# Sliding-window attention and highway layer on one core: a list-scheduled order of the pieces, one ring of two-bank PSUM buffers, x transposed by DMA, masks and normalising by head pairs

## The chip, the core and the metric

One core of one Trainium2 chip runs the whole program. The metric is device time in microseconds (us). Engines are named as in the profile: PE (matmul) with PEld (its weight loads), DVE, ACT, POOL, and SP, which here only issues DMAs. Each engine works through its own instructions in the order in which they were written, and waits at an instruction until what it needs is done.

## What is computed

Eight batches, eight heads, 576 positions, head size 64; the attention output, with the heads side by side, is the input x of a highway layer over 4608 rows of 512.

```python
scores = scale * np.matmul(q, k.transpose(0, 1, 3, 2))
bias = slopes[:, None, None] * (-np.abs(rel).astype(np.float32))[None, :, :]
mask = (rel >= 0) & (rel < window)          # rel = query - key, window = 128
scores = np.where(mask, scores + bias[None], -1000000000.0)
attn = softmax(scores)
x = (attn @ v), heads side by side: [B * S, H * D]
H = np.maximum(x @ w_h, 0.0)
T = 1.0 / (1.0 + np.exp(-(x @ w_t + b_t)))
out = T * H + (1.0 - T) * x
```

## The kernel before

**Tiling.** Two batches form a *pair* m (0 to 3). A pair has two *stages*: s = 0 covers its first 256 queries, s = 1 the other 320 (with a tail of 64). A *unit* u is one head of one stage, for both batches: 4 x 2 x 8 = 64 units. The eight stages are also numbered st = 0 to 7. A *block* b is 128 rows of x; an even stage has four, an odd one five (the fifth holds both tails), 36 in all.

**A unit's chain.** `transposes` (L188) brings q and k of two heads (a group hp, 16 transposes on PE into one `pt` tile) into QT and KT, copied by DVE (q, L204) and ACT (k, L209); a fifth group does the tails (L218). `scores` (L236, matmuls L254) fills a two-bank PSUM tile `sc` (two of them), `soft` (L264) takes the exponential on ACT, `mask` (L273) multiplies by a 0/1 mask with the distance factor on DVE. `pv` (L290) multiplies with v, which has a column of ones behind it, into `av`, and `norm` (L315, L316) divides by that column's sum into x, on DVE. `av` has one buffer.

**A block's chain.** `f_xt`: four PE transposes of x (L326) into a `pt` tile, of which there is one for all transposes in the kernel, copied to `xt` by ACT (L332). `f_h`: four matmuls with w_h (L340) and, on DVE, `uu = max(h, 0) - x` (L344). `f_z`: four matmuls with w_t (L353) and one that adds the bias from a single row (L355), tanh on ACT (L358), and `tt = 0.5 tt + 0.5` on POOL (L359). `f_g`: `uu = uu * tt` on DVE (L364), called the gate product below. `f_out`: `ot = uu + x` on POOL (L368), then four (or two) stores issued by SP (L380, L374).

**Order.** A loop written out by hand (L415 to L459) sets one order for all engines. Slot u writes the exponential of unit u, the scores of u + 1, the mask of u - 1, a share of the previous stage's block steps, product and norm of u - 2, more block steps, and from the sixth slot of a pair on one transpose group of the next pair. The gate product and the sum of a block are written one step after its z. POOL also issues all loads (they convert float32 to bfloat16): those of pair 0 and the weights first, then those of pair m + 1 in the first nine slots of pair m. At most eight of POOL's loads are in flight: the next issue waits for the eighth before it.

Of the kernel before, what the change touches and what calls it, by code (L numbers as in the profile page):

```python
# [10 lines left out]
P = 128  # L11
# [3 lines left out]
def kernel(  # L15
# [10 lines left out]
    nc = tc.nc  # L26
    B, H, S, D = q.shape
# [13 lines left out]
    NU = ND * 2 * H  # L41
# [4 lines left out]
    p0p = ctx.enter_context(tc.tile_pool(name="p0", bufs=11))  # L46
    p1p = ctx.enter_context(tc.tile_pool(name="p1", bufs=4))
    smp = ctx.enter_context(tc.tile_pool(name="small", bufs=4))
    xp = ctx.enter_context(tc.tile_pool(name="x", bufs=2))
    fx = ctx.enter_context(tc.tile_pool(name="fx", bufs=3))  # L50
# [47 lines left out]
    def load_v(m, cs):  # L98
# [11 lines left out]
    load_qk(0, slice(0, 2))  # L110

    ident = cp.tile([P, P], BF16, name="ident")
    nc.vector.memset(ident[:], 1.0)
    nc.gpsimd.affine_select(
        out=ident[:], in_=ident[:], compare_op=ALU.is_equal, fill=0.0,
        base=0, pattern=[[1, P]], channel_multiplier=-1,
    )
    kk_i = cp.tile([P, 1], I32, name="kk_i")
    nc.gpsimd.iota(kk_i[:], pattern=[[0, 1]], base=0, channel_multiplier=1)

    load_v(0, (0, 1))
    load_qk(0, slice(2, 4))
    load_qk(0, slice(4, 8))


    M0 = cp.tile([P, H, 512], BF16, name="m0")
    M1 = cp.tile([P, H, 512], BF16, name="m1")
    tri = cp.tile([P, 3, P], BF16, name="tri")
    nc.vector.memset(tri[:], 1.0)
    nc.gpsimd.affine_select(  # L130
        out=tri[:, 0, :], in_=tri[:, 0, :], compare_op=ALU.is_ge, fill=0.0,
        base=0, pattern=[[1, 4], [4, 32]], channel_multiplier=-1,
    )
    nc.gpsimd.affine_select(
        out=tri[:, 1, :], in_=tri[:, 1, :], compare_op=ALU.is_ge, fill=0.0,
        base=-1, pattern=[[-1, 4], [-4, 32]], channel_multiplier=1,
    )
    nc.gpsimd.affine_select(
        out=tri[:, 2, 0:D], in_=tri[:, 2, 0:D], compare_op=ALU.is_ge, fill=0.0,
        base=-1, pattern=[[-1, D]], channel_multiplier=1,  # L140
    )
    nc.gpsimd.affine_select(
        out=tri[:, 2, D:P], in_=tri[:, 2, D:P], compare_op=ALU.is_ge, fill=0.0,
        base=0, pattern=[[1, D]], channel_multiplier=-1,
    )
    kk_f = cp.tile([P, 1], F32, name="kk_f")
    nc.vector.tensor_copy(out=kk_f[:], in_=kk_i[:])
    BIAS = cp.tile([P, H], F32, name="bias")
    for h in range(H):
        nc.vector.tensor_scalar(  # L150
            out=BIAS[:, h : h + 1], in0=kk_f[:, 0:1],
            scalar1=slopes[h], scalar2=None, op0=ALU.mult,
        )
    hb = lambda n: [P, H, n]

    def bc(ap, n):
        return ap.rearrange("p (o n) -> p o n", o=1).to_broadcast(hb(n))

    for off in (0, 256):
        nc.vector.tensor_copy(out=M0[:, :, off : off + P], in_=bc(tri[:, 0, :], P))  # L160
    for off in (0, 256):
        nc.vector.tensor_copy(out=M1[:, :, off : off + P], in_=bc(tri[:, 0, :], P))
    nc.vector.tensor_copy(out=M1[:, :, 448:512], in_=bc(tri[:, 2, D:P], D))
    for h in range(H):
        c_h = float(np.exp(-float(P) * slopes[h]))
        for M, off, n, s in ((M0, 128, P, 1), (M0, 384, P, 1), (M1, 128, P, 1), (M1, 384, D, 2)):
            nc.vector.tensor_scalar(  # L167
                out=M[:, h, off : off + n], in0=tri[:, s, 0:n],
                scalar1=c_h, scalar2=None, op0=ALU.mult,
            )  # L170
    for i in range(2):
        nc.vector.memset(VA[i][:, :, :, :, D : D + 1], 1.0)
        nc.vector.memset(VA[i][D:P, 4, :, :, :], 0.0)
        nc.vector.memset(KT[i][:, :, S : 5 * P], 0.0)
    ones1 = cp.tile([1, P], BF16, name="ones1")
    nc.vector.memset(ones1[:], 1.0)

    load_tails(0)
    wH = cp.tile([P, NCK, DM], BF16, name="wH")
    wT = cp.tile([P, NCK, DM], BF16, name="wT")  # L180
    bT = cp.tile([1, DM], BF16, name="bT")
    nc.gpsimd.dma_start(out=wH[:], in_=moe_w_h.rearrange("(c p) n -> p c n", p=P))
    nc.gpsimd.dma_start(out=wT[:], in_=moe_w_t.rearrange("(c p) n -> p c n", p=P))
    nc.gpsimd.dma_start(out=bT[:], in_=moe_b_t.rearrange("(o n) -> o n", o=1))
    load_v(0, (2, 3, 4))
# [303 lines left out]
```

## Time and profile before

| | us |
|---|---|
| median of three runs | 243.84 |
| lowest, highest | 243.78, 250.88 |
| the profiled execution | 247.06 |
| its span, first to last instruction | 245.3 |

The span is what the views of the profile divide up; the small rest of an execution lies around it. In rows that group instructions, the fields are: line, engine, operation, tiles written and read, count, then busy us and mean ns of one, then the idle time of the engine ahead of them and what ended it. Rows of the waits: the waiting engine and line, what it waited for, us in total, times, longest. Rows in order of time: start, duration, engine, line and operation, with idle time and its cause in brackets. Matmuls overlap in the pipeline, so what one costs is read from start to start.

### The profile page before, as it was taken

The page shows a single profiled execution, that of the slowest core. Times are in us where ns is not written, and L with a number is a line of the kernel's source. Part 1 is how long each engine was busy: PE and PEld are TensorE (multiplying, and loading weights), DVE is VectorE, ACT ScalarE, POOL GpSimd, SP SyncE. Part 2 cuts the span into 40 slices and gives each one's busy share as a digit, 9 for nine tenths or more (in the row PEclk, how much of TensorE's full clock was granted, in tenths as well). Part 3 has the DMA queues.
Part 4 walks back from the last instruction along what each step waited for, and adds up shares of the span by engine and source line. Part 5 has one row for each costly group of instructions (what it writes and reads, how often), then busy time and mean ns, then how long its engine had stood idle before and what let it go on. Part 6 is the DMA issues. An engine that isn't in the chain of part 4 may idle for free.

```text
span 245.3 us, 5032 instructions
## 1 busy us (share of the span) xinstructions
PE 177.5 (72%) x2004; PEld 96.5 (39%) x2004; DVE 142.1 (58%) x339; ACT 126.3 (51%) x157; POOL 119.1 (49%) x139
## 2 busy tenths in 40 slices
PE   1355702498898777868887986888887997887980
PEld 1133402376553334445533343455443344533430
DVE  4169501364677656565786575365786586785340
ACT  2324610185665756447675645646656766562440
POOL 8987733300245876531257784412233356223572
PEclk9999965556999999799999798879999999999996
DMA  5999999995019999930159999530113223122243
GB/s 61 135 191 190 167 129 198 143 108 12 6 41 157 217 199 163 104 73 17 45 81 217 208 155 127 67 74 0 45 43 77 54 56 78 43 63 69 52 112 92
DMA packets 70199, 24.97 MB, mean 102 GB/s; under 512 B 48160, under 2 KB 65568, under 8 KB 70176
## 3 DMA queue, kind: packets, MB, share of 16 engines
q0 software_dynamic: 63392, 15.21, 80.5%
q1 hardware_dynamic: 6784, 9.45, 15.3%
q8 instruction: 15, 0.25, 0.4%
q14 instruction: 8, 0.07, 0.1%
HBM read 30.41 MB, written 9.44 MB: 162 GB/s over the span
## 4 chain that ended last, share of the span: by engine, by line
POOL 34%; issue 25%; DMA 16%; DVE 9%; PE 8%; ACT 3%; SPq 2%; POOLq 1%; ACTq 0%
POOL ot L368 16%; DMA kl<-in_k_dram 8%; POOL tt L359 8%; DMA out_dram<-ot 5%; DVE uu L364 5%; POOL va L102 4%; DMA ql<-in_q_dram 3%; PE pt L197 3%; SPq L380 2%; PE av L290 2%; DVE m L167 1%; POOL ktl L93 1%; PE sc L254 1%; ACT xt L332 1%; POOL kl L73 1%
## 5 line engine op out<-in xcount | busy, mean ns | idle before, releaser
L264 ACT ACTIVATE pt<-sc,bias 128x1024 bf16<-128x1024 f32 x64 | 71.0, 1118 | 0.7 <-PE sc L254 0.7
L359 POOL TENSOR_SCALAR tt<-tt 128x512 f16<-128x512 f16 x36 | 22.2, 618 | 85.8 <-ACT tt L358 77.7
L368 POOL TENSOR_TENSOR ot<-uu,x 128x512 f32<-128x512 bf16 x36 | 44.5, 1235 | 19.6 <-DVE uu L364 16.3
L273 DVE TENSOR_TENSOR pt<-pt,m 128x1024 bf16<-128x1024 bf16 x64 | 52.2, 816 | 0.0
L364 DVE TENSOR_TENSOR uu<-uu,tt 128x512 bf16<-128x512 bf16 x36 | 15.3, 426 | 52.4 <-POOL tt L359 52.4
L290 PE MATMUL av<-va,pt 128*128 128x65 bf16 (+1 forms) x576 | 32.7, 205 | 13.8 <-DVE x L316 12.1
L358 ACT ACTIVATE tt<-pz 128x512 f16<-128x512 f32 x36 | 21.5, 597 | 39.3 <-PE pz L355 38.1
L340 PE MATMUL pa<-wH,xt 128*128 128x512 bf16 x144 | 39.8, 401 | 1.3 <-ACT xt L332 0.8
L353 PE MATMUL pz<-wT,xt 128*128 128x512 bf16 x144 | 38.9, 394 | 0.0
L290 PEld LDWEIGHTS <-pt 128*128 128x128 bf16 (+1 forms) x576 | 24.7, 105 | 33.7 <-DVE x L316 22.2
L332 ACT COPY xt<-pt 128x512 bf16<-128x512 bf16 x36 | 21.1, 586 | 31.2 <-PE pt L326 31.0
L209 ACT COPY kt<-pt 128x1024 bf16<-128x1024 bf16 x16 | 16.2, 1012 | 39.4 <-PE pt L197 39.4
L254 PE MATMUL sc<-qt,kt 64*128 64x256 bf16 (+2 forms) x384 | 29.6, 260 | 7.2 <-ACT kt L209 4.4
L316 DVE TENSOR_TENSOR x<-av,rd 128x256 bf16<-128x256 f32 (+1 forms) x64 | 29.3, 458 | 6.0 <-POOL ot L368 3.8
L197 PE MATMUL pt<-ident,ql 128*64 128x128 bf16 x256 | 13.3, 255 | 22.5 <-DMA ql<-in_q_dram 13.4
L102 POOL DMA_DIRECT2D va<-in_v_dram x20 | 22.2, 1113 | 12.6 <-DMA kl<-in_k_dram 4.5
L344 DVE SCALAR_TENSOR_TENSOR uu<-pa,x 128x512 bf16<-128x512 f32 x36 | 24.6, 682 | 5.3 <-PE pa L340 5.3
L326 PE MATMUL pt<-ident,x 128*128 128x128 bf16 x144 | 15.2, 228 | 8.4 <-DVE qt L204 4.2
L254 PEld LDWEIGHTS <-kt 64*128 64x128 bf16 x384 | 14.8, 100 | 15.9 <-issue 6.4
L197 PEld LDWEIGHTS <-ql 128*64 128x64 bf16 x256 | 10.6, 131 | 25.4 <-DMA ql<-in_q_dram 19.2
L204 DVE COPY qt<-pt 128x1024 bf16<-128x1024 bf16 x16 | 11.0, 689 | 15.2 <-PE pt L197 15.2
L340 PEld LDWEIGHTS <-xt 128*128 128x128 bf16 x144 | 11.7, 100 | 15.4 <-issue 4.5
(45 smaller groups left out, 129.1 us busy)
## 6 DMA issues: line engine op xcount, KB each, us to landing
out_dram<-ot SPq DMA_DIRECT2D x128, 64.0 KB, 1.7
va<-in_v_dram POOLq DMA_DIRECT2D x16, 256.0 KB, 8.7
ql<-in_q_dram POOLq DMA_DIRECT2D x3, 1024.0 KB, 11.1
kl<-in_k_dram POOLq DMA_DIRECT2D x3, 1024.0 KB, 12.3
out_dram<-ot SPq DMA_DIRECT2D x8, 128.0 KB, 2.4
ql<-in_q_dram POOLq DMA_DIRECT2D x4, 128.0 KB, 4.8
kl<-in_k_dram POOLq DMA_DIRECT2D x4, 128.0 KB, 5.3
ql<-in_q_dram POOLq DMA_DIRECT2D x2, 256.0 KB, 7.2
```

What stands on the lines that cost most here:

```text
L102: nc.gpsimd.dma_start(out=VA[i][0:n, c, :, :, 0:D].rearrange("s r h d -> s (r h) d"), in_=v[2 * m : 2 * m + 2, :, c * P : c * P + n, :].re ...
L197: nc.tensor.transpose(out=pt[r * D : (r + 1) * D, hl * 512 + t * P : hl * 512 + (t + 1) * P], in_=L[:, r, 2 * hp + hl, t * D : (t + 1) * D ...
L254: nc.tensor.matmul(out=sc[:, r, off : off + w], lhsT=KT[i][rows, h, j * P : (j + 1) * P], rhs=rhs, start=True, stop=True,)
L264: nc.scalar.activation(out=pt[:], in_=SC.pop(u)[:], func=ACTF.Exp, bias=BIAS[:, h : h + 1], scale=scale,)
L273: nc.vector.tensor_tensor(out=pt[:], in0=pt[:], in1=mk.to_broadcast([P, 2, 512]), op=ALU.mult,)
L290: nc.tensor.matmul(out=av[rows, g, :], lhsT=pt[:, r, off : off + w], rhs=va[:, j, r, h, :], start=n == 0, stop=n == len(terms) - 1,)
L316: nc.vector.tensor_tensor(out=x[:, 0:nb, h * D : (h + 1) * D], in0=av[:, 0:nb, 0:D], in1=rd[:, 0:nb].to_broadcast([P, nb, D]), op=ALU.mult,)
L340: nc.tensor.matmul(out=pa[:], lhsT=xt[:, c, :], rhs=wH[:, c, :], start=c == 0, stop=c == NCK - 1)
L353: nc.tensor.matmul(out=pz[:], lhsT=xt[:, c, :], rhs=wT[:, c, :], start=c == 0, stop=False)
L359: nc.gpsimd.tensor_scalar(out=tt[:], in0=tt[:], scalar1=0.5, scalar2=0.5, op0=ALU.mult, op1=ALU.add)
L364: nc.vector.tensor_tensor(out=uu[:], in0=uu[:], in1=TT.pop((st, b))[:], op=ALU.mult)
L368: nc.gpsimd.tensor_tensor(out=ot[:], in0=UU.pop((st, b))[:], in1=X[st][:, b, :], op=ALU.add)
```

## The change

**Order.** The hand-written loop goes. Every piece of work (a transpose group, its copy, the scores, the exponential, a mask, a product, a norm, each step of a block, each load, each constant) becomes a node with an engine, a cost in ns, a due time (units are due 2300 ns apart) and the nodes that it needs. A list scheduler in the kernel's Python keeps a clock for each engine and takes, again and again, the piece that can start first; among those that can start within 100 ns of the first on an engine it takes the one due first. It models loads (bytes per ns, eight in flight) and the PSUM ring. The resulting order is written out. A load is issued when its buffer is free in that model and POOL comes to it.

**PSUM.** One ring of four two-bank buffers `ps` serves scores, products, transposes (q in one bank, k in the other, so one buffer for both) and blocks (h in one bank, z in the other), taken strictly in order.

**x by DMA.** `f_x` issues one DMA transpose of a block, 128x512 bf16, from x to `xt`, on SP; the PE transposes L326 and the copies L332 are gone. `xt` has five buffers, x three, `ot` four of its own.

**Pairs.** Mask, product and norm work on two heads (w = u // 2): 32 masks of 128x2048 in place of 64 of 128x1024, 32 norms in place of 64, 32 reciprocals. One mask table `mk` serves both stages. The bias matmul uses 128 rows, of which all but the first are zero. Setup moves: ident and tri to POOL alone, the distance bias to ACT, and four of pair 0's five k copies from ACT to DVE.

Three places in the order. DVE, in the first stage of pair 1: before, masks (L273) of one head, norms (L315, L316) and the gate products (L364) alternate.

```order
L364 TENSOR_TENSOR uu<-uu,tt 128x512
L273 TENSOR_TENSOR pt_1006<-pt_1006,m_124 128x1024
L315 RECIPROCAL rd<-av 128x4
L316 TENSOR_TENSOR x<-av,rd 128x4x64
L273 TENSOR_TENSOR pt_1054<-pt_1054,m_124 128x1024
L344 SCALAR_TENSOR_TENSOR uu<-pa,x 128x512
```

And now (L298 is the mask, L342 and L343 the norm, L368 the `uu` of h, L393 the gate product):

```order
L368 SCALAR_TENSOR_TENSOR uu<-ps,x 128x512
L342 RECIPROCAL rd<-ps 128x2x4
L343 TENSOR_TENSOR x<-ps,rd 128x2x4x64
L298 TENSOR_TENSOR pt_907<-pt_907,mk 128x2048
L393 TENSOR_TENSOR uu<-uu,tt 128x512
L298 TENSOR_TENSOR pt_965<-pt_965,mk 128x2048
L368 SCALAR_TENSOR_TENSOR uu<-ps,x 128x512
```

The pieces are twice as long, and where the gate product stands between them follows from the scheduler's clocks instead of a fixed lag of one step.

POOL, from the first tt on, before (L359 and L368 are tt and ot, the rest are loads of pair 2):

```order
L359 TENSOR_SCALAR tt<-tt 128x512
L368 TENSOR_TENSOR ot<-uu,x 128x512
L73 DMA ql_91<-in_q_dram 128x16x256
L359 TENSOR_SCALAR tt<-tt 128x512
L368 TENSOR_TENSOR ot<-uu,x 128x512
L73 DMA kl_93<-in_k_dram 128x16x256
```

And now (L388 and L397 are tt and ot; ql_82 to ktl_88 and va_90 belong to pair 2, ql_83 and kl_85 to pair 3):

```order
L388 TENSOR_SCALAR tt<-tt 128x512
L397 TENSOR_TENSOR ot<-uu,x 128x512
L75 DMA ql_82<-in_q_dram 128x16x256
L75 DMA kl_84<-in_k_dram 128x16x256
L95 DMA qtl_86<-in_q_dram 64x8x64 x2
L95 DMA ktl_88<-in_k_dram 64x8x64 x2
L388 TENSOR_SCALAR tt<-tt 128x512
L75 DMA ql_83<-in_q_dram 128x16x256
L397 TENSOR_TENSOR ot<-uu,x 128x512
L75 DMA kl_85<-in_k_dram 128x16x256
L388 TENSOR_SCALAR tt<-tt 128x512
L104 DMA va_90<-in_v_dram 128x16x64 x2
```

Pair 2's and pair 3's loads of q and k now stand among the first three blocks.

SP, from its start, now:

```order
L353 DMA_TRANSPOSE xt<-x 128x4x128 x4
L413 DMA out_dram<-ot 32x512 x8
L353 DMA_TRANSPOSE xt<-x 128x4x128 x3
L413 DMA out_dram<-ot 32x512 x4
L353 DMA_TRANSPOSE xt<-x 128x4x128 x2
```

Where SP held stores alone, each block's transpose now stands among the stores of earlier blocks.

The core of the diff:

```diff
-    ps_sc = ctx.enter_context(tc.tile_pool(name="ps_sc", bufs=2, space=PSUM))
-    ps_tr = ctx.enter_context(tc.tile_pool(name="ps_tr", bufs=1, space=PSUM))
-    ps_av = ctx.enter_context(tc.tile_pool(name="ps_av", bufs=1, space=PSUM))
-    ps_a = ctx.enter_context(tc.tile_pool(name="ps_a", bufs=1, space=PSUM))
-    ps_z = ctx.enter_context(tc.tile_pool(name="ps_z", bufs=1, space=PSUM))
+    NPS = 4
+    psp = ctx.enter_context(tc.tile_pool(name="ps", bufs=NPS, space=PSUM))
+    def ps_tile(dt=F32):
+        return psp.tile([P, 2, 512 if dt == F32 else 1024], dt, name="ps")
...
+    EV = {
+        (m, w, hp): "ACT" if w and (m or hp == 0) else "DVE"
+        for m in range(ND) for w in (0, 1) for hp in range(5)
+    }
...
-        pt = ps_tr.tile([P, 1024], BF16, name="pt")
+        if w == 0:
+            TR[m, hp] = ps_tile(BF16)
+        pt = TR[m, hp][:, w, :]
...
+    def mask(w):
+        m, s, h = unit(2 * w)
+        n = 2 - s
+        o = PT[w][:].rearrange("p h r (j w) -> p h (r j) w", j=n)
+        mk = MK[:, h : h + 2, 0 : 512 // n].rearrange("p h (o w) -> p h o w", o=1)
+        nc.vector.tensor_tensor(
+            out=o, in0=o, in1=mk.to_broadcast([P, 2, 2 * n, 512 // n]), op=ALU.mult,
+        )
...
+        av = AV.pop(w)[:, :, 0 : nb * (D + 1)].rearrange("p h (b d) -> p h b d", b=nb)
+        rd = smp.tile([P, 2, 5, 1], F32, name="rd")
+        nc.vector.reciprocal(out=rd[:, :, 0:nb], in_=av[:, :, :, D : D + 1])
+        nc.vector.tensor_tensor(
+            out=x.rearrange("p b (h d) -> p h b d", h=2), in0=av[:, :, :, 0:D],
+            in1=rd[:, :, 0:nb].to_broadcast([P, 2, nb, D]), op=ALU.mult,
         )
...
-    def f_xt(st, b):
-        pt = ps_tr.tile([P, 1024], BF16, name="pt")
-        for c in range(NCK):
-            nc.tensor.transpose(
...
+    def f_x(st, b):
         xt = fx.tile([P, NCK, P], BF16, name="xt")
         XT[st, b] = xt
+        nc.sync.dma_start_transpose(out=xt[:], in_=X[st][:, b, :])
     def f_h(st, b):
         xt = XT[st, b]
-        pa = ps_a.tile([P, DM], F32, name="pa")
+        az = ps_tile()
+        pa, PZ[st, b] = az[:, 0, :], az[:, 1, :]
...
+    def node(key, eng, cost, prio, emit, deps=(), take=False, free=None, land=0):
...
+            for b in range(nb):
+                t = base + b * dt
+                kb = (st, b)
+                node(("x", kb), "SP", 700, t - 1.3 * dt, lambda kb=kb: f_x(*kb), alln, land=0.01)
+                node(("h", kb), "PE", 870, t, lambda kb=kb: f_h(*kb), [("x", kb), ("w", 0)], take=True)
+                node(("u", kb), "DVE", 690, t + 0.2 * dt, lambda kb=kb: f_u(*kb), [("h", kb)], free=("h", kb))
+                node(("z", kb), "PE", 1100, t + 0.5 * dt, lambda kb=kb: f_z(*kb), [("h", kb), ("w", 1), ("w", 2)])
+                node(("th", kb), "ACT", 600, t + 0.6 * dt, lambda kb=kb: f_th(*kb), [("z", kb)], free=("h", kb))
+                node(("t", kb), "POOL", 630, t + 0.6 * dt, lambda kb=kb: f_t(*kb), [("th", kb)])
+                node(("g", kb), "DVE", 430, t + 0.9 * dt, lambda kb=kb: f_g(*kb), [("u", kb), ("t", kb)])
+                node(("o", kb), "POOL", 1200, t + 1.0 * dt, lambda kb=kb: f_out(*kb), [("g", kb)])
...
+        if land and e == "POOL":
+            t = max(t, lanes[0] + SYNC)
+        if take and len(slots) >= NPS:
+            left, at = allocs[slots[-NPS]]
+            if left:
+                return None
+            t = max(t, at + SYNC)
...
+            t0 = min(c[0] for c in cands)
+            soon = [c for c in cands if c[0] <= t0 + LOOK]
+            c = min(soon, key=lambda c: c[1])
...
+    order.sort(key=lambda o: o[0])
     with tc.manual_schedule():
...
+        for t, key in order:
+            nodes[key][3]()
```

More of the change, by code (lines that the diff above doesn't have):

```diff
@@ L138 @@
[L138 to L170, printed above, removed]
@@ L309, in norm @@
+        if s == 1:
+            for hl in range(2):
+                for r in range(2):
+                    group(hl, 4, r, ((me, 384, 3), (me, 448, 4)), slice(r * D, (r + 1) * D))
+    def norm(w):
+        m, s, h = unit(2 * w)
         nb = NBLK[s]
@@ new lines, with start_of @@
+    ready = {e: [] for e in clock}
+    for key, nd in nodes.items():
+        if not waiting[key]:
+            ready[nd[0]].append(key)
+    def start_of(key):
+        e, cost, prio, emit, deps, take, free, land = nodes[key]
+        t = clock[e]
+        for d in deps:
+            t = max(t, when[d] + (0 if nodes[d][0] == e and not nodes[d][7] else SYNC))
+        if land and e == "POOL":
[5 more added lines that the diff above has]
+            t = max(t, at + SYNC)
+        return t
```

436 lines of the change are left out of this document (264 added, 172 removed).

## Prediction

> **What bounds the kernel now.** I read the page's engine line first, then busy time by stage, then who waits for whom on the busiest engines, then the start and end of the program in order of time.
>
> ```profile
> span 245.3 us, 5032 instructions
> PE 177.5 (72%) x2004; PEld 96.5 (39%) x2004; DVE 142.1 (58%) x339; ACT 126.3 (51%) x157; POOL 119.1 (49%) x139
> ```
>
> No engine is full over the span, so the average names no bound. Cut into start, middle and end (busy time by stage: PE, weight loads, DVE, ACT, POOL, then granted clock, DMA share, GB/s):
>
> ```profile
> 0.00:62.00 62.00, 30.70 (x405) 21.53 (x405) 27.54 (x96) 22.89 (x24) 31.42 (x45) 0.78 1.93 132
> 62.00:230.00 168.00, 138.47 (x1567) 71.61 (x1562) 110.03 (x235) 99.22 (x127) 79.21 (x85) 0.96 0.66 91
> 230.00:245.30 15.30, 8.32 (x43) 3.33 (x40) 4.53 (x9) 4.15 (x7) 8.48 (x10) 0.84 0.39 94
> ```
>
> Start and end leave PE more than half or almost half idle. In the middle 168 us PE is busy 138.5 and idle 29.5. The waits of that stretch, DVE's first, then PE's:
>
> ```profile
> DVE uu L364 <- POOL tt L359: 44.9, 31, 2.9
> DVE x L316 <- POOL ot L368: 3.8, 4, 1.0
> DVE uu L344 <- PE pa L340: 3.2, 4, 1.7
> DVE qt L204 <- PE pt L197: 2.8, 3, 1.2
> ...
> PE av L290 <- DVE x L316: 12.1, 22, 1.1
> PE pt L197 <- ACT xt L332: 5.6, 9, 0.7
> PE pt L326 <- DVE qt L204: 3.9, 4, 1.6
> PE pt L326 <- DVE qt L225: 3.9, 2, 1.9
> ```
>
> DVE's busy 110.0 plus these waits of 54.7 make 164.7 of 168: DVE, in its written order, sets the pace there, and 45 us of its time is standing at the gate product (L364) until POOL has made tt, with masks and norms behind it that are ready. PE's idle time is the echo: 12.1 us for the norm that frees the only `av` buffer, 13.4 us for the only `pt` buffer of all transposes.
>
> The start is a second bound:
>
> ```profile
> 30.19 0.36 PE L290 MATMUL av<-va,pt 128*128 128x65 bf16 x6
> 40.52 1.06 PE L197 MATMUL pt<-ident,ql 128*64 128x128 bf16 x16 [9.97 <-DMA ql<-in_q_dram]
> 46.21 1.06 PE L197 MATMUL pt<-ident,kl 128*64 128x128 bf16 x16 [2.38 <-DMA kl<-in_k_dram]
> ...
> 50.00:54.00 4.00, 4.00 (x66) 3.39 (x63) 3.26 (x9) 3.31 (x5) 0.00 (x0) 0.50 4.57 126
> 54.00:58.00 4.00, 3.75 (x53) 2.93 (x50) 2.58 (x5) 2.22 (x3) 0.00 (x0) 0.50 1.86 25
> 58.00:62.00 4.00, 3.33 (x45) 2.06 (x43) 1.51 (x4) 2.84 (x4) 0.00 (x0) 0.80 0.01 0
> ```
>
> PE stops for pair 1's q at 30.5 and really starts with its k at 46.2 (each after its load). It then runs at a granted clock of 0.50 although busy 7.75 of the 8 us from 50 to 58; the next 4 us have 0.80, so half speed lasts until about 59.
>
> **The change part by part.** The start: the loads ahead of pair 1's k are the same bytes, in nearly the same order (six q/k pieces for pair 0 become four, q and k each). POOL now makes ident and tri ahead of the second pieces; these are some 2 us of POOL, and the loads queue eight deep behind it. I keep 46.2, with 44 to 49 as ends. The new order has scores of fifteen of pair 0's units, six of its eight head-pair products with v and the first gate block on PE ahead of pair 1's transposes, where before seven units and no block stood; that work fills the 10 us hole, and leaves less for afterwards. Cover gone (pair 1 arriving earlier), it would cost its own time and the sum would not change.
>
> PE's work after 46.2, by its pace in a stretch where it hardly waits. Each row's start to the next row's start is the cost:
>
> ```profile
> 67.45 0.64 PE L197 MATMUL pt<-ident,ql 128*64 128x128 bf16 x16 [0.67 <-ACT xt L332]
> 68.02 0.40 PE L254 MATMUL sc<-qt,kt 64*128 64x256 bf16 x8
> 68.35 1.04 PE L353 MATMUL pz<-wT,xt 128*128 128x512 bf16 x4
> 69.32 0.39 PE L355 MATMUL pz<-bT,ones 1*128 1x512 bf16 x1
> 69.64 0.60 PE L290 MATMUL av<-va,pt 128*128 128x65 bf16 x12
> 70.07 0.62 PE L197 MATMUL pt<-ident,kl 128*64 128x128 bf16 x16
> 70.62 0.39 PE L254 MATMUL sc<-qt,kt 64*128 64x256 bf16 x4
> 70.94 1.04 PE L340 MATMUL pa<-wH,xt 128*128 128x512 bf16 x4
> ```
>
> A gate block is 0.97 (h, the same as z) + 0.97 + 0.32 = 2.26 us; the wider bias operand (128 rows, 127 of them zero) I cost like the old one, since it has the same 512 columns. 35 blocks: 79.1. Scores of 49 units x 0.33 = 16.2. Probabilities times v: a head pair is 12 matmuls in an even stage (0.43) and 24 in an odd one (0.86); 12 and 14 of them: 17.2. Transposes: 20 groups of 16 x 0.56 = 11.2 (pair 1's four q groups run before 46.2), and six tails at half a group, an estimate, 1.7. Sum 125.4 us. What is no longer in it is the transposition of x:
>
> ```profile
> L326 PE MATMUL pt<-ident,x 128*128 128x128 bf16 x144 | 15.2, 228 | 8.4 <-DVE qt L204 4.2 <-DVE qt L225 3.9 <-DVE x L316 0.3
> L332 ACT COPY xt<-pt 128x512 bf16<-128x512 bf16 x36 | 21.1, 586 | 31.2 <-PE pt L326 31.0
> ```
>
> 15.2 us of PE, its 8.4 us of waits and 21.1 us of ACT. ACT falls to about 105 us, and bounds nothing.
>
> DVE, by rows that keep shapes apart:
>
> ```profile
> L273 DVE TENSOR_TENSOR pt<-pt,m 128x1024 bf16<-128x1024 bf16 x64 | 52.2, 816 | 0.0
> L316 DVE TENSOR_TENSOR x<-av,rd 128x320 bf16<-128x320 f32 x32 | 15.7, 491 | 2.1 <-POOL ot L368 0.9
> L364 DVE TENSOR_TENSOR uu<-uu,tt 128x512 bf16<-128x512 bf16 x36 | 15.3, 426 | 52.4 <-POOL tt L359 52.4
> L316 DVE TENSOR_TENSOR x<-av,rd 128x256 bf16<-128x256 f32 x32 | 13.6, 424 | 3.9 <-POOL ot L368 2.9
> L315 DVE RECIPROCAL rd<-av 128x5 f32<-128x5 f32 x32 | 5.9, 185 | 0.9 <-PE av L290 0.8
> ```
>
> Norm: 64 more columns cost 67 ns, so a pair of 640 columns is 491 + 335 = 826 against 982, one of 512 is 692 against 848, and one of two reciprocals of about 0.18 goes: 0.3 us a pair, 32 pairs, 10 us. Mask by pairs: the row's mean of 816 mixes undisturbed masks of 0.68 with some of 1.27, which begin while POOL works:
>
> ```profile
> 107.66 1.27 DVE L273 TENSOR_TENSOR pt<-pt,m 128x1024 bf16<-128x1024 bf16 x1
> 109.54 0.68 DVE L273 TENSOR_TENSOR pt<-pt,m 128x1024 bf16<-128x1024 bf16 x1
> ```
>
> Against the 0.43 of the 512-column product L364, twice the columns cost 0.25 more undisturbed, so a pair is between 0.68 + 0.50 = 1.18 (14 us saved in all, from 816) and 1.63 (nothing). I take 1 us, near the dear end, since DVE will not decide. Setup saves a few us, and four of pair 0's k copies come from ACT (4 us): even. DVE has about 131 us, some 30 of it before 46 (27.5 were done in the first 62 us, and more of pair 0 is done early now), so about 101 after it: under PE's 125.4 if its standing goes. With 45 us of it kept, 146: 46 + 146 + 7 = 199. The gate product now stands behind other work by the list order, so I take half of that standing away and PE as the bound.
>
> Added: 36 transposes by DMA on SP, in one queue with the output stores, which wait for POOL's ot. A late ot holds the next stage's transposes behind its store, and PE's h waits for those; the order asks for them more than a block ahead. No DMA transpose is in this trace. The nearest rows:
>
> ```profile
> q0 software_dynamic: 63392, 15.21, 80.5%
> out_dram<-ot SPq DMA_DIRECT2D x128, 64.0 KB, 1.7
> ```
>
> One packet holds one of 16 engines for 0.805 x 16 x 245.3 / 63392 = 50 ns. A block is 128 KB: in 256 B rows 512 packets, 1.6 us; in 64 B pieces 2048 packets, 6.4 us. I take 3.2 us (128 B), which 4.5 us of block time hides. The Trainium skill, "VectorE: DVE Perf Modes", The three transpose paths, speaks against the move: it gives 1309 ns for 128x128 by DMA and 390 ns on TensorE, and advises TensorE where PSUM will do; four in series would be 5.24 us a block by that estimate. No run here shows the DMA's side.
>
> Sum: 46.2 + 125.4 + 6 (13 us at half clock) + waits of PE + the end. The end:
>
> ```profile
> 238.09 0.39 PE L355 MATMUL pz<-bT,ones 1*128 1x512 bf16 x1
> ```
>
> From 238.5 to 245.3 runs the last block's tanh, POOL, gate, sum and store: 6.8, unchanged. PE's waits lie between 0 and the 29.5 of before: I take 15, since both single buffers go, but a ring of four, taken in order, is new. 46.2 + 125.4 + 6 + 15 + 6.8 = 199.4 us of span. The profiled execution took 247.06 about its span of 245.3, the runs' median is 243.84, so a median is 0.994 of a span: **198 us**. The Trainium skill, "TensorE: Matmul & The Clock Gate", Part 1: The HAM clock gate, has the clock released after about 3.4 us of sustained activity; by that, as an estimate, the clock's term would be 1.7 and the time 194. The rows above show 0.50 for 12 us, so the 6 stays.
>
> **The rivals.**
> - The plan holds nearly as written, no waits on PE: 46.2 + 125.4 + 6 + 6.8 = 184.4, a median of 183. For it: ACT and DVE have slack. Against it: every queue is in order, and landing times vary.
> - The waits only move. POOL's list has the loads of pairs 2 and 3 among its first ten blocks, closer than before; an issue waits until the eighth load before it has landed, and the next tt and ot stand behind it, then DVE's gate product, then masks. Or the ring: a score tile waits for a transpose tile whose k half comes later. With all 29.5 us kept: 214, a median of 213.
> - The order is no better, the DVE stall stays and its cover too: 242 to 245. Against it: the removed PE and ACT work is certain.
> - The DMA transposes set the pace, one after another, T each. The first is issued by 40.5 (its block stands ahead of pair 1's q on PE), and after the last come 2.26 + 6.8: 40.5 + 36 T + 9.1. From T = 4.2 this passes 200, and from **T = 5.4** the kernel is slower than before; at 64 B pieces (6.4) it takes 280. At T between 4.2 and 5.4 it is 201 to 244. For it: nothing in the trace prices it. Against it: stores of 64 KB land in 1.7 us. By the figure of the Trainium skill above ("VectorE: DVE Perf Modes", The three transpose paths) T is 5.24 and the time 238, a median of 237; that lies in the case with T under 5.4.
>
> **How the numbers follow.** Forecast 198 (190 to 208) 0.50; plan as written 183, 0.10; waits moved 213, 0.22; order no better 243, 0.04; transposes set the pace, under 5.4 us each (about 225) 0.06, over it (about 280) 0.08. The range 184 to 222 holds the first three but for their edges, 0.8. About 2% can be told apart here: faster 0.88 (forecast, plan, moved waits, the milder transposes), within 2% 0.04, slower 0.08.
>
> **What would show it.** Right: PE busy near 160 us in all and above 0.85 of the time after 62; DVE's wait for tt (44.9) at a third or less; ACT about 105; transposes landing in under 4.5 us; pair 1's k transposed at 44 to 49 and the clock 0.5 until about 60. Wrong: h (L360) waiting for DMA for more than 20 us in all; POOL's load issues idle for more than 15 us after 50; PE idle over 35 us after 62; DVE over 140 us busy.

## The result and the profile after

The changed kernel takes **222.87 us**, the median of 4 runs (220.11 to 227.69), and the kernel before 245.49 us in the same job (243.78 to 250.88): a ratio of 0.903, with a 95% interval of 0.884 to 0.922. It is faster by 22.6 us, where the forecast had 46. The profiled execution took 221.99 us around a span of 220.3. Medians and ranges are of all executions; the ratios and their intervals leave out those more than 1.5% above their kernel's fastest, and two profiles that fell in such an execution, of own banks with x on PE (222.30 us) and of the transposes issued by ACT (365.16 us), are not read.

The head of the page of the changed kernel, then its busy time by stage (PE, weight loads, DVE, ACT, POOL, granted clock, DMA share, GB/s). The DMA share adds up the time of all packets over that of 16 engines, so packets that are under way together can take it past 1.

```profile
span 220.3 us, 4642 instructions
PE 154.5 (70%) x1837; PEld 88.3 (40%) x1860; DVE 130.0 (59%) x214; ACT 102.9 (47%) x125; POOL 125.8 (57%) x137
```

```profile
0.00:46.00 46.00, 24.66 (x340) 17.95 (x343) 25.24 (x48) 18.65 (x25) 28.33 (x41) 0.93 1.57 144
46.00:62.00 16.00, 12.63 (x204) 8.33 (x200) 7.72 (x15) 7.30 (x9) 9.44 (x11) 0.79 3.16 143
62.00:100.00 38.00, 26.62 (x310) 14.20 (x312) 19.35 (x31) 18.74 (x23) 22.84 (x23) 0.87 1.64 196
100.00:140.00 40.00, 30.66 (x350) 16.07 (x357) 26.38 (x40) 20.02 (x23) 21.19 (x21) 0.87 1.64 127
140.00:180.00 40.00, 35.26 (x427) 19.26 (x432) 31.28 (x51) 26.62 (x32) 21.54 (x20) 1.00 0.42 92
180.00:200.00 20.00, 16.43 (x185) 9.19 (x186) 14.93 (x24) 8.60 (x11) 12.71 (x13) 1.00 0.55 116
200.00:220.30 20.30, 8.24 (x35) 3.28 (x36) 5.14 (x10) 2.98 (x5) 9.77 (x11) 0.88 0.46 110
```

PE and ACT have lost the work that the forecast took from them (177.5 to 154.5, 126.3 to 102.9), and DVE 12 us. But PE is busy only 70% and 77% of the time from 62 to 140, and 88% from 140 to 180. From 62 on, the two poor stages are those in which the DMA share is 1.64; where it has fallen to 0.42, PE runs well. The waits (engine, line, what it waited for: us in all, times, longest):

```profile
ACT tt L384 <- DVE uu L368: 59.4, 27, 8.6
DVE uu L393 <- POOL tt L388: 29.7, 18, 9.0
...
PE ps L360 <- DMA xt<-x: 21.3, 8, 5.6
...
POOL va L104 <- DMA kl<-in_k_dram: 12.6, 2, 7.0
```

Three rows answer to those of before. DVE's standing at the gate product, 52.4 us over the whole span before, is 29.7. PE has a wait that it did not have, 21.3 us for x transposed by DMA. And tanh waits 59.4 us for the `uu` of h, on which it does not depend in the mathematics.

Its DMA rows (queues: packets, MB, share of 16 engines; issues: KB, median us to landing):

```profile
q1 hardware_dynamic: 26368, 14.17, 35.1%
...
kl<-in_k_dram POOLq DMA_DIRECT2D x3, 1024.0 KB, 21.9
...
xt<-x SPq DMA_TRANSPOSE x36, 4.1
```

The median of 4.1 us mixes two groups. For the 18 transposes that are issued up to 129, and then for the 18 from 145 on (least, median, longest):

```profile
DMA to landing us min/median/max: 4.3/8.5/10.6
```

```profile
DMA to landing us min/median/max: 2.4/2.5/3.9
```

The last of POOL's loads lands at 136. While loads are under way, a transpose takes more than three times as long as after them.

The loads of k of pairs 1 to 3 land in a median of 21.9 us, 12.3 before. Not all of that is the transposes' doing: the new order sets the loads of pairs 2 and 3 close together, and with x on PE, without a DMA transpose, the median is 19.0. Pair 1's own k took 20.3 us before, issued at 25.82, and takes 21.9 now, issued at 28.84. How late it is, and what slow landings do, is seen on PE in order of time where pair 1 arrives, and a little later on three engines at once (start, duration, engine, line; in brackets the idle time ahead of it and who ended it):

```profile
41.91 0.61 PE L360 MATMUL ps<-wH,xt 128*128 128x512 bf16 x1 [3.78 <-DMA xt<-x]
...
50.76 2.14 PE L213 MATMUL ps<-ident,kl 128*64 128x128 bf16 x48 [1.85 <-DMA kl<-in_k_dram]
```

```profile
76.46 1.89 PE L360 MATMUL ps<-wH,xt 128*128 128x512 bf16 x4 [4.65 <-DMA xt<-x]
...
77.75 1.14 POOL L104 DMA_DIRECT2D va<-in_v_dram  x1 [6.95 <-DMA kl<-in_k_dram]
...
80.03 0.62 POOL L388 TENSOR_SCALAR tt<-tt 128x512 f16<-128x512 f16 x1
...
80.68 0.42 DVE L393 TENSOR_TENSOR uu<-uu,tt 128x512 bf16<-128x512 bf16 x1 [9.05 <-POOL tt L388]
```

Pair 1's k is transposed at 50.76 instead of 46.21: 3.0 us by the later issue, 1.5 by the longer landing. At 77.75 a load of v has stood 6.95 us on POOL until k had landed; the tt behind it comes at 80.03, and DVE has stood 9.05 us for it: this is the rival of the moved waits. Meanwhile PE stood 4.65 us for xt, and then four matmuls of the gate take 1.89 us instead of the 1.04 that they took at 68.35 in the kernel before.

### The profile page after: what moved, and what is told of

It is laid out like the page before. It is cut to its first block, busy times and chain, and to the rows that moved or that the text cites. A ratio compares the mean times of both kernels' runs of the same rounds, so it can differ in the third digit from the quotient of the medians.

```text
span 220.3 us, 4642 instructions
## 1 busy us (share of the span) xinstructions
PE 154.5 (70%) x1837; PEld 88.3 (40%) x1860; DVE 130.0 (59%) x214; ACT 102.9 (47%) x125; POOL 125.8 (57%) x137
## 3 DMA queue, kind: packets, MB, share of 16 engines
q1 hardware_dynamic: 26368, 14.17, 35.1%
## 4 chain that ended last, share of the span: by engine, by line
DMA 41%; PE 16%; DVE 12%; POOL 12%; ACT 7%; issue 6%; SPq 4%; POOLq 1%; ACTq 0%
DMA xt<-x 10%; DMA ktl<-in_k_dram 9%; DMA va<-in_v_dram 9%; DMA kl<-in_k_dram 9%; PE ps L377 6%; PE ps L360 5%; ACT pt L287 5%; DVE uu L368 5%; POOL ot L397 4%; DMA out_dram<-ot 4%; DVE pt L298 4%; SPq L413 3%; POOL tt L388 2%; ACT tt L384 2%; PE ps L213 2%
## 5 line engine op out<-in xcount | busy, mean ns | idle before, releaser
L287 ACT ACTIVATE pt<-ps,bias 128x1024 bf16<-128x1024 f32 x64 | 67.8, 1117 | 17.1 <-PE ps L277 17.1
L360 PE MATMUL ps<-wH,xt 128*128 128x512 bf16 x129 | 39.6, 409 | 26.6 <-DMA xt<-x 21.3
L397 POOL TENSOR_TENSOR ot<-uu,x 128x512 f32<-128x512 bf16 x36 | 46.4, 1289 | 20.6 <-DVE uu L393 19.5
L384 ACT ACTIVATE tt<-ps 128x512 f16<-128x512 f32 x36 | 21.6, 599 | 72.6 <-DVE uu L368 59.4
L298 DVE TENSOR_TENSOR pt<-pt,mk 128x2048 bf16<-128x2048 bf16 x32 | 43.1, 1346 | 6.7 <-ACT pt L287 6.7
L388 POOL TENSOR_SCALAR tt<-tt 128x512 f16<-128x512 f16 x36 | 28.5, 791 | 32.0 <-ACT tt L384 25.6
L368 DVE SCALAR_TENSOR_TENSOR uu<-ps,x 128x512 bf16<-128x512 f32 x36 | 24.8, 690 | 36.8 <-PE ps L379 23.3
L377 PE MATMUL ps<-wT,xt 128*128 128x512 bf16 x136 | 39.7, 413 | 1.8 <-DVE uu L368 1.2
L393 DVE TENSOR_TENSOR uu<-uu,tt 128x512 bf16<-128x512 bf16 x36 | 16.1, 446 | 29.8 <-POOL tt L388 29.7
L277 PE MATMUL ps<-qt,kt 64*128 64x256 bf16 (+2 forms) x384 | 25.6, 258 | 7.8 <-ACT tt L384 4.0
L314 PE MATMUL ps<-va,pt 128*128 128x65 bf16 (+1 forms) x576 | 25.1, 202 | 6.0 <-DVE pt L298 3.3
L360 PEld LDWEIGHTS <-xt 128*128 128x128 bf16 x144 | 12.5, 102 | 40.4 <-DMA xt<-x 24.6
L343 DVE TENSOR_TENSOR x<-ps,rd 128x512 bf16<-128x512 f32 (+1 forms) x32 | 24.3, 758 | 1.1
L377 PEld LDWEIGHTS <-xt 128*128 128x128 bf16 x144 | 13.9, 104 | 18.4 <-issue 7.0
## 6 DMA issues: line engine op xcount, KB each, us to landing
kl<-in_k_dram POOLq DMA_DIRECT2D x3, 1024.0 KB, 21.9
```

The lines of the kernel that those rows point to most:

```text
L277: nc.tensor.matmul(out=sc[:, r, off : off + w], lhsT=KT[i][rows, h, j * P : (j + 1) * P], rhs=rhs, start=True, stop=True,)
L287: nc.scalar.activation(out=PT[u // 2][:, h % 2], in_=SC.pop(u)[:], func=ACTF.Exp, bias=BIAS[:, h : h + 1], scale=scale,)
L298: nc.vector.tensor_tensor(out=o, in0=o, in1=mk.to_broadcast([P, 2, 2 * n, 512 // n]), op=ALU.mult,)
L314: nc.tensor.matmul(out=av[rows, hl, g * (D + 1) : (g + 1) * (D + 1)], lhsT=pt[:, hl, r, off : off + k_], rhs=va[:, j, r, h0 + hl, :], star ...
L343: nc.vector.tensor_tensor(out=x.rearrange("p b (h d) -> p h b d", h=2), in0=av[:, :, :, 0:D], in1=rd[:, :, 0:nb].to_broadcast([P, 2, nb, D ...
L360: nc.tensor.matmul(out=pa, lhsT=xt[:, c, :], rhs=wH[:, c, :], start=c == 0, stop=c == NCK - 1)
```

## The experiments

All ratios are to the kernel before, timed in the same job. Where the order is planned anew, a difference holds the new order too. Short names: "x on PE" transposes x on TensorE as before the change; "own banks" takes h and z out of the shared two-bank tile; "paced loads" holds back the loads of pairs 2 and 3.

### How much of the gain is one step of lag

The kernel before, with one number changed, so that the gate product and the output sum are emitted two steps after z instead of one:

```diff
-            late.append((clock[0] + 1, lambda: (f_g(st, b), f_out(st, b))))
+            late.append((clock[0] + 2, lambda: (f_g(st, b), f_out(st, b))))
```

> The kernel before with the gate product and the sum written two steps after z in place of one, nothing else. If DVE's standing at the gate product (44.9 us from 62 to 230) set the pace, most of it goes and the time falls to 225 to 235. If PE's single buffers (av, pt) set it and DVE's wait only filled the gap: 240 to 246.

Measured: 226.93 us (226.01 to 227.80), ratio 0.927 (0.919 to 0.936). Its waits of DVE from 62 to 230:

```profile
DVE uu L364 <- POOL tt L359: 5.7, 6, 1.9
```

The standing of 44.9 us is 5.7, and the time falls by 18.6 us, four fifths of what the whole change brings. So the reading of the profile before was right: DVE's place in front of the gate product was the bound. And it is a warning: scheduler, ring, DMA transposes and merged norms together bring only 4 us more than that one step.

### x on PE again, in the new order

```diff
+        pt = ps_tile(BF16)
+        XP[st, b] = pt
+        for c in range(NCK):
+            nc.tensor.transpose(
+                out=pt[:, 0, c * P : (c + 1) * P],
+                in_=X[st][:, b, c * P : (c + 1) * P], identity=ident[:],
+            )
+    def f_xc(st, b):
+        pt = XP.pop((st, b))
         xt = fx.tile([P, NCK, P], BF16, name="xt")
-        nc.sync.dma_start_transpose(out=xt[:], in_=X[st][:, b, :])
+        nc.scalar.copy(
+            out=xt[:], in_=pt[:, 0, 0:512].rearrange("p (c n) -> p c n", c=NCK)
+        )
```

The scheduler plans the transposes on PE (400 ns) and the copy on ACT (590 ns) in place of the DMA.

> The changed kernel with x transposed on PE again (four PE transposes into a buffer of the ring, copy to xt by ACT), the order planned anew. Theory DMA (the missing 20 us are the transposes by DMA: they wait behind loads, and slow the loads): PE's 21 us of waits for xt go, loads end earlier, PE pays 14 us, ACT 21: 208 to 215. Theory tile (the missing time is the shared PSUM tile of h and z, which chains z, uu and tanh): nothing of that changes, and PE and ACT work comes on top: 225 to 232.

Measured: 214.55 us (213.97 to 215.11), ratio 0.877 (0.870 to 0.884). Its engines' busy time, around a span of 213.4 us:

```profile
PE 158.5 (74%) x1979; PEld 94.2 (44%) x2004; DVE 128.8 (60%) x214; ACT 120.8 (57%) x161; POOL 118.6 (56%) x137
```

ACT works 18 us more and PE 4 us more (busy; part of its work runs at a higher clock now), and the kernel is 8.3 us faster by the medians, 5.0 at the least (the fastest run of the change, 220.11, against 215.11). The part of the change that takes most work away from the engines costs time.

### Is it the waiting for xt, or the traffic?

The same kernel with x on PE, which also issues the 36 DMA transposes on SP, into a tile that nobody reads:

```diff
+        xd = dm.tile([P, NCK, P], BF16, name="xd")
+        nc.sync.dma_start_transpose(out=xd[:], in_=X[st][:, b, :])
```

> The kernel of the run with x transposed on PE, in the same order, with 36 DMA transposes of x added on SP whose result nobody reads. Theory contention (the transposes and the loads hold each other up in the DMA engines): loads land later, pair 1's k at 50 or later, 218 to 222. Theory latency (only the wait of h for its own transpose costs time): nothing waits for these, 214 to 216.

Measured: 219.91 us (219.55 to 220.49), ratio 0.904 (0.897 to 0.911), against 214.55 without them. PE where pair 1's k arrives, with x on PE alone, and then with the unread transposes:

```profile
48.41 2.77 PE L213 MATMUL ps<-ident,kl 128*64 128x128 bf16 x48 [0.51 <-DMA kl<-in_k_dram]
```

```profile
50.97 2.77 PE L214 MATMUL ps<-ident,kl 128*64 128x128 bf16 x48 [1.56 <-DMA kl<-in_k_dram]
```

Nobody reads what these transposes write, and yet 5.4 of the 8.3 us are there: k comes 2.6 us later. What the 5.4 us consist of besides the late k was not taken apart. The transposes also stand on SP ahead of the stores, and POOL stands 5.1 us in two places until one has landed. They show the two groups again: three of them are issued while no load is under way, from 108.6 to 118, and land in 2.5 to 3.8 us; the four between 120 and 133, beside loads, take over 7 and up to 10.5. The rest of the 8.3, some 3 us by the medians, is not resolved: the runs of the change begin at 220.11 and those with unread transposes at 219.55, and the two kernels differ in the work of PE and ACT as well. What waiting for xt costs beyond the traffic is therefore not shown.

### Is it the plan's number for the landing?

The change, planned with 1200 ns of SP and 4000 ns to landing instead of 700 and 2500:

```diff
-                node(("x", kb), "SP", 700, t - 1.3 * dt, lambda kb=kb: f_x(*kb), alln, land=0.01)
+                node(("x", kb), "SP", 1200, t - 1.3 * dt, lambda kb=kb: f_x(*kb), alln, land=0.01)
...
-                when[key] = t + cost + 2500
+                when[key] = t + cost + 4000
```

> The changed kernel, planned with a DMA transpose of 1200 ns of SP and 4000 ns to landing in place of 700 and 2500 (measured: 1214, and 4.1 us from issue). Theory latency: with the true length in the plan PE's 21 us of waits for xt fall under 8, 208 to 216. Theory contention: while loads run the landing is 5 to 10 us whatever the plan says, waits of 15 to 25 us stay, 218 to 224.

Measured: 226.44 us (225.75 to 228.98), ratio 0.932 (0.919 to 0.946); not better, and by its range rather worse. Its PE wait for xt, beside a median landing of 2.9 us:

```profile
PE ps L360 <- DMA xt<-x: 17.7, 6, 3.9
```

The median in the plan does not help: a later h shortens the wait by 3.6 us and gives the time away elsewhere. A plan with the 8 to 10 us that a transpose takes beside loads was not tried, so whether the scheduler asks for xt too late there stays open.

### The DMA transposes alone, in the kernel before

```diff
-        pt = ps_tr.tile([P, 1024], BF16, name="pt")
...
-        nc.scalar.copy(
-            out=xt[:], in_=pt[:, 0:512].rearrange("p (c n) -> p c n", c=NCK)
-        )
+        nc.sync.dma_start_transpose(out=xt[:], in_=X[st][:, b, :])
```

> The kernel before with x transposed by DMA on SP, nothing else: 15 us of PE, 21 us of ACT and the waits for the shared pt buffer go. Theory DMA: transposes issued one step ahead land in 4 us and more while loads run, so h waits for them; 240 to 255. If the transposes are as good as hidden: 228 to 238.

Measured: 346.11 us (342.51 to 347.26), ratio 1.412 (1.397 to 1.428). It takes the transposes off PE and the copies off ACT like the change (15.2 and 21.1 us), and loses 100 us. The transposes land quickly, in a median of 2.5 us, and yet PE waits 102.0 us for xt. One turn of the loop, in order of time (L347 is the end of z, L350 tanh, L351 tt, L356 the gate product, L360 ot, L372 its store, L326 the next transpose of x, L332 the next h):

```profile
284.31 0.39 PE L347 MATMUL pz<-bT,ones 1*128 1x512 bf16 x1
284.79 0.60 ACT L350 ACTIVATE tt<-pz 128x512 f16<-128x512 f32 x1 [8.08 <-PE pz L347]
285.48 0.62 POOL L351 TENSOR_SCALAR tt<-tt 128x512 f16<-128x512 f16 x1 [9.00 <-ACT tt L350]
...
286.13 0.42 DVE L356 TENSOR_TENSOR uu<-uu,tt 128x512 bf16<-128x512 bf16 x1 [1.90 <-POOL tt L351]
286.64 1.15 POOL L360 TENSOR_TENSOR ot<-uu,x 128x512 f32<-128x512 bf16 x1 [0.54 <-DVE uu L356]
287.82 2.69 SPq L372 DMA_DIRECT2D out_dram<-ot  x4
...
290.61 1.20 SPq L326 DMA_TRANSPOSE xt<-x  x1
...
293.07 1.44 PE L332 MATMUL pa<-wH,xt 128*128 128x512 bf16 x4 [2.85 <-DMA xt<-x]
```

On SP the transpose at 290.61 stands behind the stores of 287.82, these wait for ot, ot for the gate product, and that for z. So h at 293.07 does not start before an earlier block is through, 8.8 us after that block's last z, and PE stands for it; a gate block is 2.26 us of PE. It is the order of SP's queue, which the prediction named, and then trusted the lead of a block to cover.

The same kernel with the transposes issued by ACT:

```diff
-        nc.sync.dma_start_transpose(out=xt[:], in_=X[st][:, b, :])
+        nc.scalar.dma_start_transpose(out=xt[:], in_=X[st][:, b, :])
```

> The kernel before with x transposed by DMA, but issued by ACT, so that no transpose stands behind the stores on SP, which wait for ot. Theory SP order (in the run with SP each transpose waits for the block before it to be finished): 346 falls to 235 to 260. Theory slow DMA (the transposes themselves are slow): it stays over 300.

Measured: 264.44 us (256.77 to 365.16), against 244.54 of the kernel before; no ratio is given. So by the medians 82 of the 100 us go with another queue, as SP's order has it; the one run of 365.16 stands apart from the other three, which reach 264.67. Why it is still some 20 us behind the kernel before was not found out.

### The shared tile of h and z, and the pace of the loads

In the change h and z are the two halves of one two-bank tile. A block of the change in order of time:

```profile
142.39 0.38 PE L379 MATMUL ps<-bT,ones 128*128 128x512 bf16 x1
...
142.81 0.69 DVE L368 SCALAR_TENSOR_TENSOR uu<-ps,x 128x512 bf16<-128x512 f32 x1 [0.31 <-PE ps L379]
...
143.59 0.60 ACT L384 ACTIVATE tt<-ps 128x512 f16<-128x512 f32 x1 [1.59 <-DVE uu L368]
```

`uu` reads only h, which was complete before z began, but starts after z's last matmul (142.77); tanh reads only z, and starts after `uu`. The two readers of one tile run in series, 0.8 us late each block. The scheduler's graph has no such edge: there `uu` needs h, and tanh needs z.

Own banks: h and z in one-bank tiles of their own, and a ring of three instead of four in the six banks left. That is two edits in one; the banks don't allow the first alone. (The scheduler also learns that the next block's h waits for this one's `uu`, and its z for tanh, since each tile has one buffer.)

```diff
-    NPS = 4
+    NPS = 3
...
+    ps_a = ctx.enter_context(tc.tile_pool(name="ps_a", bufs=1, space=PSUM))
+    ps_z = ctx.enter_context(tc.tile_pool(name="ps_z", bufs=1, space=PSUM))
...
-        az = ps_tile()
-        pa, PZ[st, b] = az[:, 0, :], az[:, 1, :]
+        pa = ps_a.tile([P, DM], F32, name="pa")[:]
...
-        pz = PZ[st, b]
+        pz = ps_z.tile([P, DM], F32, name="pz")[:]
+        PZ[st, b] = pz
```

> The changed kernel with h and z in PSUM tiles of their own, one bank each, and a ring of three for the rest, the order planned anew. Theory tile: uu follows h and tanh follows z without each other, so tanh's 59 us of waits for uu and uu's 23 us for z go, ring buffers come free earlier, PE waits 10 to 15 us less: 206 to 212. Theory DMA: PE still stands over 20 us for xt, 217 to 224; a ring of three can cost a few us.

Measured: 223.31 us (222.11 to 227.46), ratio 0.911 (0.898 to 0.924): nothing gained. The two rows of its waits:

```profile
ACT tt L387 <- PE pz L382: 71.1, 28, 9.1
```

```profile
PE pa L362 <- DMA xt<-x: 24.1, 9, 7.0
```

Tanh no longer waits for DVE, but stands as long for z itself, and PE still stands 24.1 us for xt.

Paced loads: the loads of pair m, from pair 2 on, wait for the exponentials of the first units of the pair before, nine steps in all (two q, two k, five v).

```diff
+    def at(m, r):
+        return [("exp", 2 * H * (m - 1) + r)] if m > 1 else []
...
-                   [("tr", m - 2, w, hp) for hp in range(4)], cost=1200)
+                   [("tr", m - 2, w, hp) for hp in range(4)] + at(m, w), cost=1200)
```

> The changed kernel, with the loads of pairs 2 and 3 held until the exponentials of the pair before reach their first nine units, as before the change. Theory contention: the stretch from 60 to 120 is no longer full of loads, transposes land in about 3 us, PE waits for xt 10 us less, POOL's issues block tt less: 212 to 217. Theory latency: 219 to 224.

Measured: 222.39 us (219.26 to 224.98), against 247.71 of the kernel before in its job; no ratio is given. Nothing by itself either; PE's wait for xt is 25.1 us in it. Then the edits by twos and threes, put together from the same lines:

> x transposed on PE, and h and z in PSUM tiles of their own with a ring of three. Theory tile: with the DMA's waits out of the way the chain z, uu, tanh is what is left, and undoing it gives 204 to 210. If the shared tile costs nothing net: 213 to 217.

> x transposed on PE, h and z in tiles of their own, and the loads of pairs 2 and 3 held back as before the change. Theory POOL (early loads keep POOL's tt behind issues that wait for landings, DVE stands 7 to 9 us once at the gate product): 198 to 203. If the pacing is of no account, as in the run with the held loads alone: 203 to 208.

> The change with x transposed on TensorE (214.6 us alone) and the loads of pairs 2 and 3 paced (222.4 alone, no gain), the shared two-bank tile of h and z kept. Theory A, pacing pays as soon as the DMA transposes are gone, whatever the tile: 206 to 208 us, the 8 us that pacing gave to the kernel with own banks. Theory B, pacing pays only where h and z also have banks of their own, since tanh's wait for DVE would take the freed time: 212 to 216 us, and ACT's wait for DVE's uu (29 us before) stays at 25 or more.

> The change with own one-bank tiles for h and z (223.3 us alone) and the loads paced (222.4 alone), x still transposed by DMA. Theory A, the DMA transposes are what swallows both gains: 218 to 224 us, PE's waits for xt still over 20 us. Theory B, pacing and own banks are enough, since paced loads leave the DMA engines to the transposes: 203 to 208 us, PE's waits for xt under 12 us.

All eight combinations (median us; ratio to the kernel before, its 95% interval):

| | x by DMA | x on PE |
|---|---|---|
| as in the change | 222.87; 0.903 (0.884, 0.922) | 214.55; 0.877 (0.870, 0.884) |
| own banks | 223.31; 0.911 (0.898, 0.924) | 204.92; 0.835 (0.822, 0.848) |
| paced loads | 222.39; no ratio | 210.29; 0.861 (0.856, 0.867) |
| both | 220.28; 0.892 (0.883, 0.902) | **197.11**; 0.812 (0.806, 0.818) |

With x by DMA neither edit nor both bring more than 3 us. With x on PE own banks bring 9.6, paced loads 4.3, both 17.4, more than their sum. So the DMA transposes hide the two other faults. With them PE's wait for xt stays in each version, 24.1, 25.1 and 25.7 us against 21.3; these 3 to 4 us more are not all of the hidden gain, and where the rest of it goes was not taken apart. The waits of both edits with x by DMA, then of paced loads with x on PE:

```profile
PE pa L362 <- DMA xt<-x: 25.7, 9, 6.2
```

```profile
ACT tt L396 <- DVE uu L380: 13.1, 11, 2.1
```

The shared tile's wait is smaller there by itself (29.3 us with x on PE alone). Its time, 210.29, fell between what both theories had expected of it (206 to 208, and 212 to 216): pacing pays with the shared tile too, 4.3 us, but about half of the 7.8 with own banks. Why is not settled.

The best version, x on PE with own banks and paced loads, runs 197.11 us (196.73 to 197.31). Its busy time by stage and PE's longest wait from 46 to 200:

```profile
46.00:62.00 16.00, 10.83 (x184) 8.40 (x185) 7.67 (x13) 8.67 (x11) 8.73 (x8) 0.79 2.91 154
62.00:187.00 125.00, 118.88 (x1451) 66.97 (x1450) 93.23 (x150) 93.46 (x123) 83.01 (x85) 0.99 0.86 118
187.00:195.30 8.30, 0.38 (x2) 0.00 (x0) 0.88 (x3) 0.60 (x1) 3.37 (x4) 0.72 0.40 99
```

```profile
PE ps L216 <- DVE qt L237: 4.0, 1, 4.0
```

PE is busy 95% of the time from 62 to 187 at a clock of 0.99: now PE is the bound, as the prediction wanted it, although it transposes x itself.

## Why the prediction was half right

The direction and its reason held; the gain was half of what the sum gave, and the median lies 0.9 us above the range's upper end. (By the ratio of 0.903, the 243.84 of before become 220.1, inside it.)

- **The bound before: right.** One step of lag, and nothing else, takes the standing from 44.9 to 5.7 us and the time down by 18.6.
- **PE's work: right, its clock not.** 125.4 and 6 us for the half clock were forecast after 46.2; the rows from 46 on sum to 129.8. Two differences cancel in that. The half clock took 10 us (below). And some of the gate's matmuls have no record, as the counts show, which should be 144 and 144:

```profile
L360 PE MATMUL ps<-wH,xt 128*128 128x512 bf16 x129 | 39.6, 409 | 26.6 <-DMA xt<-x 21.3
...
L377 PE MATMUL ps<-wT,xt 128*128 128x512 bf16 x136 | 39.7, 413 | 1.8 <-DVE uu L368 1.2
```

  The 23 that are missing are about 5 us, an estimate from the 0.97 of four. 129.8 and 5, less 10, is 125.
- **ACT and DVE: right.** ACT 102.9 for about 105, DVE 130.0 for about 131. Norm and reciprocal came out as worked out; the masks, taken at 1 us, gave more:

```profile
L298 DVE TENSOR_TENSOR pt<-pt,mk 128x2048 bf16<-128x2048 bf16 x32 | 43.1, 1346 | 6.7 <-ACT pt L287 6.7
...
L343 DVE TENSOR_TENSOR x<-ps,rd 128x512 bf16<-128x512 f32 (+1 forms) x32 | 24.3, 758 | 1.1
```

  The masks fell from 52.2 to 43.1, with 1.35 us a pair inside the forecast 1.18 to 1.63. That DVE's total still came out is luck: the masks gave 8 us more than was taken, and most of that is missing elsewhere. It decided nothing, as forecast.
- **The waits of PE, 15 us: the step that failed.** From 46 until its last matmul ends, PE is idle 35.7 us by its records (220.3 less 46, less 8.8 of the end, less 129.8 busy), so some 30 when the missing matmuls are counted as work. 17.5 of it are waits for xt (21.3 less the 3.78 at 41.91, ahead of 46). The rest includes pair 1's k, at 50.76 for the forecast 44 to 49. The prediction priced a transposition at one length, 3.2 us, hidden by 4.5 us of block time. Measured, there are two lengths: 2.5 us in the half that is issued after the loads, and 8.5 in the half that runs beside them, which 4.5 us do not hide. Three of the waits after 46, 12.8 us, are for transposes of that half. The other four, 4.7 us from 197 on, come at landings of 2.4 to 2.5 us; there all but the first transpose stand on SP between the stores of earlier blocks, which the prediction had named. Nor had it priced that the transposes delay the loads in turn: the unread transposes cost 5.4 us, with all that they do.
- **The end, 6.8 us: 8.8 measured**, from the end of PE's last matmul (211.50) to 220.3. The last block:

```profile
211.12 0.38 PE L379 MATMUL ps<-bT,ones 128*128 128x512 bf16 x1
211.53 0.69 DVE L368 SCALAR_TENSOR_TENSOR uu<-ps,x 128x512 bf16<-128x512 f32 x1 [1.25 <-PE ps L379]
...
212.32 0.60 ACT L384 ACTIVATE tt<-ps 128x512 f16<-128x512 f32 x1 [1.34 <-DVE uu L368]
```

  `uu` and tanh run in series there too, 0.8 of the 2 us; "unchanged" overlooked what one tile for two readers does. With own banks the best version has 7.9.
- **The sum closes:** by the records, 20.7 us more waits, 2 more at the end and 1.6 less work are the 21 us by which the span of 220.3 exceeds the forecast 199.4. The median exceeds the forecast 198 by 4 us more than that: the factor of 0.994 came from a profiled execution that was slower than its kernel's median, and here the median is 1.012 of the span.
- **The rivals.** Waits that move came true in part (POOL's load at 77.75 and DVE behind it). The transposes cost time, but not as their rival had it, one after another at a length that sets the pace: SP issues the next one after 1.2 to 1.9 us, while the last is still under way. They cost it together with the loads, which the prediction had in another rival. Of the signs against it, the first came (21.3 us of h waiting for DMA, over the 20 named). PE idle over 35 us after 62 came as well: the rows from 62 leave 41.1 idle, or 32 without the end. And POOL's issues of loads stand 20 us after 50, over the 15 named. Of the signs for it, PE's share after 62 (0.74, for over 0.85) and pair 1's k did not come; ACT's 103 did.
- **The standing at the gate product:** half of it was to go; over the whole span 29.7 of 52.4 us are left, 57%. The sign had a third.

Taking away the three faults that the experiments found brings 197.11 us, beside a forecast of 198. PE is idle 11.3 us after 46 in that kernel (187.38 less 46, less the 130.1 busy in the rows above), so the 15 was the size of a good order's waits, not of this one's. That the two times agree is in part luck: in that kernel PE also transposes x, which the forecast had taken off it.

The clock's term was 6 us, once. After 46, the granted clock of the changed kernel is 0.50 throughout in four stretches:

```profile
51.50:58.32 6.82, 6.28 (x69) 4.01 (x65) 0.85 (x2) 4.28 (x5) 6.12 (x7) 0.50 4.21 135
71.98:82.22 10.24, 5.76 (x37) 2.76 (x38) 1.54 (x3) 2.39 (x3) 4.43 (x5) 0.50 1.80 160
102.70:106.11 3.41, 3.41 (x31) 1.43 (x27) 2.02 (x5) 1.01 (x1) 1.78 (x2) 0.50 3.90 105
126.59:133.42 6.83, 5.04 (x22) 2.31 (x24) 0.51 (x1) 1.14 (x2) 0.45 (x1) 0.50 2.16 152
```

PE is busy 20.5 us in them, and at half clock half of that is lost: 10 us for the 6 forecast. The first stretch was forecast, and is shorter than before; it loses 3. The other three each lie at one of PE's long waits for xt (4.65 us until 76.46, 2.57 until 101.44, 5.63 until 128.16). In the second, PE starts again at 76.46 and works without a gap at 0.50 until 82.22. The best version has a mean of 0.99 from 62 to 187. So a wait of PE seems to cost more here than its own length, though no experiment sets the two apart. The Trainium skill, "TensorE: Matmul & The Clock Gate", Part 1: The HAM clock gate, has the clock released after a busy window of about 3.4 us, in windows that run freely; work that starts within one would by that, as an estimate, stay at half clock for up to twice as long. The 5.8 us from 76.46 to 82.22 fit that; the 12 of before, with PE busy 7.75 of the 8 us from 50 to 58, are longer.

## What to carry to other kernels

Work that moves from a compute engine to the DMA queues is not free because the engine's share falls: price the landing under the loads that run at that time, what it does to those loads, and what it stands behind in its queue. An edit that changes nothing may be hidden by another wait: three edits that give 8.3, -0.4 and 0.5 us singly give 25.8 together, so try them in combination before dropping one. A median can hide two groups, here 2.5 and 8.5 us: look at a cost by stage before it goes into a sum. And when one line of the old kernel brings most of a rewrite's gain, the rest of the rewrite has to be tested part by part.

## What the runs showed of the hardware

- A DMA transpose of a 128x512 block in bf16 takes SP 1.19 us or more to issue. In the change it lands in 4.3 to 10.6 us while POOL's loads are under way, and in 2.4 to 3.9 after the last of them. The Trainium skill, "VectorE: DVE Perf Modes", The three transpose paths, has 1309 ns for 128x128, 5.24 us for four in series by an estimate; the traces don't show that series, since a whole block lands in 2.5 us. The same page's advice, under Rules for kernel authors, to use TensorE where PSUM will do is borne out by 8.3 us.
- Each such transpose is 544 packets, (26368 - 6784) / 36, and its packets take about 1.1 us of all 16 engines, if the stores' take what they took before: 35.1% of 220.3 us less 15.3% of 245.3, over 36. The prediction had 1.6 to 6.4 us.
- One queue's order can cost more than the work in it: 100 us for 36 transposes behind stores on SP, 82 of them gone by another queue, by the medians.
